# Early loads and Q projections in another order, copies of x also on ScalarE, and a new order table, in a cached attention kernel on one core

## The chip, the core and the metric

The kernel runs on one core of a Trainium2 chip. The core has TensorE (PE, matrix multiplications), VectorE (DVE), ScalarE (ACT), GpSimd (POOL) and SyncE (SP, which here issues all transfers). They run side by side and wait for each other on semaphores. TensorE writes into PSUM, which has eight banks; VectorE and ScalarE copy from there into SBUF. The metric is device time in microseconds (us) of one execution; lower is better. A profile is a recording of one execution.

## The reference: two attention blocks with a cache

Two independent problems, A and B, of the same shape, whose results are put side by side:

```python
q = (x @ wq).reshape(B, Sq, Hq, Dh).transpose(0, 2, 1, 3)
k = jnp.repeat(k_cache, rep, axis=1)          # rep = 2
v = jnp.repeat(v_cache, rep, axis=1)
scores = jnp.einsum("bhqd,bhkd->bhqk", q, k) * (Dh ** -0.5)
p = softmax(scores, axis=-1)
o = jnp.einsum("bhqk,bhkd->bhqd", p, v)
out = o.transpose(0, 2, 1, 3).reshape(B, Sq, Hq * Dh) @ wo
```

B = 16 batches, Sq = 80 new positions, D = 576, Hq = 32 query heads on Hkv = 16 key heads, Sk = 512 cached positions, Dh = 128. All inputs are bf16. K and V are 16 x 16 x 512 x 128 each, per problem.

## The kernel before

**Units.** The work is cut into 128 units, 64 for each problem. A unit is one batch and four key heads (eight query heads, so 640 query rows on 4 x 512 keys). Eight batches make a half. Eight units with the same key heads and the same half are an octet (`goct`); octets are walked in pairs, a unit of one and a unit of the other in turn.

**Steps of a unit.** K is loaded for two units at a time by a transposing transfer (L637, `ldk`), V for one unit (L641, `ldv`). Scores are five matmul groups: four of 128 query rows, one for each key head (L684, `qk`), and one that takes the 32 rows left over of each of the four heads at once, on four 32-column parts of the array (L671, `qkr`). Each group fills one PSUM bank. VectorE takes the negated maximum (L693, `max`), ScalarE the exponential with the row sum (L697, `exp`), VectorE the reciprocal (L703, `rcp`), GpSimd multiplies (L706, `nrm`). For two units together TensorE then transposes the probabilities in 64-row parts of the array (L741, `tr`); VectorE or ScalarE copies them out (L758, L759, L767, L768: `ptev`, `prev`); the product with V follows (L789, `pv`) and is copied out (L803, `oev`). The output projection with `wo` (L835, `op`) runs over 16 heads at a time; its first part goes to an accumulator (L847), the second is added (L864) and stored (L870).

**Q projection.** For each octet there are eight steps `m`: four batches and two query heads each (`m` 0 to 3 for the first four batches, 4 to 7 for the others). A head's projection is four matmuls over the first 512 rows of `wq` (L557, `qp`) and one 64-row matmul over the last 64 rows (L570, `qt`; two heads sit on the two 64-row parts). The result is scaled and copied out (L582 on ScalarE, L583 on VectorE: `qev`). `wq` of the first two octets is loaded in four pieces of 256 columns (L526, `ldwa`), the rest whole; the last 64 rows come by two loads more (L530, `ldwt`).

**x.** In problem A, x is loaded as rows in two parts for each half (L400, `ldx`: blocks of 128 rows, three and two), transposed by TensorE block by block (L421, `xtr`) and copied out by VectorE (L426, `xev`). GpSimd repeats its last 64 columns (L408, `xrp`); they are transposed (L439, `xt`) and copied (L443, `xe`). In problem B a transposing transfer does most of it, and only the last 64 columns are loaded as rows (`ldxs`), transposed (L476, `xtt`) and copied in three instructions (L481 to L483, `xte`).

**The order.** Every operation is added with a name, the resources that it reads and writes, and a stream. Within a stream, operations keep the order of their keys. The order across streams is the table `ORDER`: one letter for the next operation of a stream (streams sorted by name), an apostrophe ahead of it where an operation that may run on VectorE or ScalarE (`alt=EV`) takes ScalarE, and a digit for the PSUM bank where a bank is taken. Each engine executes its operations in the order of that table. Waits follow from the resources. A load (a name that begins with `ld`) also waits for the TensorE operation that stands last ahead of it in the table:

```python
            if op.eng == "pe":
                last_pe = op
            elif op.paced and last_pe is not None:
                deps[id(last_pe)] = last_pe
```

All loads and stores are issued by SyncE, one after another. There are six places for K and six for V (`NK`, `NV`), 16 for probabilities, two for `wq`.

In the table before, the transfers ahead of the first K are a piece of `wq`, the first part of x, a piece of `wq` of octet 1, two `ldwt`, a piece, an `ldwt`, the second part of x, an `ldwt`, and three pieces: twelve. The second K load stands behind two pieces and a part of x, the third behind the other part of x and two V loads. Ahead of the first score matmul, TensorE has five blocks of x, eight `qp` of octet 0 and four of octet 1.

Of the kernel before, what the change touches and what calls it, by code (L numbers as in the profile page):

```python
# [7 lines left out]
F32 = mybir.dt.float32  # L8
# [26 lines left out]
X2K = 6.0  # L35
# [5 lines left out]
EV = ("dve", "act")  # L41
# [10 lines left out]
W4 = 2  # L52
# [10 lines left out]
1f6f2id7pmqmpnd0d5emppBACme'B'Amf3g1f4f7d6k0d5pqCpmnmef3f2'A'Bd1k6f5MpCppMpmmmd4k0f6k7eMMCpvvvvwOwvOvvvg37m'A'  # L63
Bmqh5012qnz'yh6ial4f3k0f5'z'ynxLpCCMpc1cf6c2cc4l7cm'um't'tf3c2icd0f1f4pLpCuppmmmd7ef2f5d3m'BCAppvvvvwvvvwvd1me
g67A'Bmqh3420Fh1nzf5f4qCpypC'yf6'xFd1nd2emzpc3cf5c7c'Am't'umif0c1d4cf7d6CppwvvvvvvwmtCpBmef1ac3c'Av'Bmh5042vpu
mf7ph3g16'y'z'xmyqf5b0c4cf7f3nqpCzCpn'tmic1cd6ic4f2cc5bcpupmmm'r'uCtCvvvwvvwvvvf3f1ad4ef2d0f7pppApm'Bmd3imeh45
61amBAh2'z'y'xig70zf3qf5f1'yFf4aic6cpnmc2Fcc7ctCqpCpp'u'tic6cb2f7'unmmbf0f5d6f1mpCrppCpmd2mmeg47d3wvvvwvvvvvBq
Amd0eh6521Bn'Aih0qy'zf4xp'yn'zf3f5f6d0c2Cpcc1cm't'uc7cc4cf2f1mCptCpppm'umvvwvvvwvmb7f3d5f4bd6ppCrmmd2mvveeg13B
'A'ABqh0475h2ib6qyy'z'xnn'zg07CCqqnac1f2bf5f3cc4pnwvvvvmrppmcf7d6d0f5ef2mpCupm'AmpBCc4cf7c3cf6ad5vvwvm't'ud2vp
tpmeh4310mBACzh7'y'xf6f2f4'zf5c1cipCytppmc3c'umc7cc0cif6b1tCpp'ummmd2f3f0iiibaf6d4d5pCpprmmvvwvvvvvvwmd7eeh163  # L70
0'BABh2A'yg74xg15q'z'zn'yf3c6cb0c7cqqqCtpn'unnmc2cf4f6bc7cf1Ctppp'ummmf2f3b5pCrbf6f1d7d4mprppCmvvvvwvvwvvd2mmd
0eeh5631CA'B'Ah4Bz'yag72'xf5'z'yqpf0ic3cc1f6cf4n'tmc7qppCpmb3f5cf0bCuptpvwvwvnmmc2f1cd6f4d7mCprpvvvvvd5m'umd0m
eaeh4123ACz'B'B'A'yih7g06'y'zf5Jf4xqc1f2cf3Jc7cinb0qpupCppn'tmmmf6bc7iCpvvvmcf4f1d2c3cf5mptpCpd6d7mvvwvwvvmd4m
ureeh0531CBC'A'Baiih2'z'A'yf4b6f7ypxpm'zmf0f2bc4cf5c1cGpCppum'r'tmvvwvvc3cf0d4f6d7f1c2icpppCum'tmmd3mwvvvvd5ee
h2160A'A'B'zBh4yg37'xg12'z'yqqnc5cf0b6c4f3ca'tnpCCqpmnmc5cf7bf1f3c0cqpuptpC'rmmn'umd4b6f7d5f2f0id3bpppCmwvvvvw
vvvvmmrd7eaieh0612'B'BAACh4'z'yg35xqf7'y'zJGif6nc1f0cc2cf4qCtppc1n'umcc3icb2f7'umtppCpmmf3d5d6f0md1f4JbpCppmmv
vvvvvvwwrCmd3eeh2407'AvBByh6'A'z'y'zag35xqf1f2c6cc4f7cf0nqCtpppb3n'ummd4f5c6f1cc2ipptCpmmmmbf6f7id0cd5pCpmvwvv
vvvvwvrCumad1eeh2367A'A'BBh4'zf0'yif1f5'z'yf3xppc6cc7m'tmcCupc2cc0cf7f4b6f1pCpvwvvwv'tmm'ud5d3f2ibd0mpppCmmm'r
vvvvd7eeah6412A'B'Bh3Ay'zg70'xg65'zqc4cf1c2cnqqpCuqb7nn'ym'tnbc6f3cf2rpCpc0b4f1iacf7i'tmm'uf6f5d2d0f3Cppmvvvwv
vmppCmbd7mpCrmd6vwvveeh3145'Ah2CBBy'A'z'y'zg70xqqf1iif3nc2cf4c5f6cnpppm'umc7cb0f1ppttCmmbf5f3Fd4ac2f6mpd7cd1pC  # L80
pmmwvvvvvwvvvurmd5eeh6023A'B'ABCyh4'zg75'xvf0'z'yqf6f2c1cc4f3caiinppqCpup'tmnc7mcb1c0cf5f4mmtCppmvvbif7d3f2d5F
d6pCprummmd4vwvvwvveeh7102CCBy'A'Ah5f6'B'z'y'zb3f7xppmmc2f1cf0f5bf6d4Fc7ppppCtmmcd0vvvvvvwm'r'umf5c2cf1iec7cd6
# [12 lines left out]
cc6cf1b5mputCmd6f4f7bimmCpppsd2d3mvvvvvwvvwvmmd0eieh4751DA'A'BBh6'yg02x'zg34'z'yqc7cc5f6cn'tc1cf0b7qqptpCn'umm
nvwvf1f2d5c6cbaf0f3ipqCCpummf6b1spCppnmmbf4d7d3vwvvvvvmspmd1eeh0624CBh7'A'A'B'zyg35'xf1'zf0yqc7ncc6cf2Cptpp'uf
4f3c7mmpmqpCmnmb6DDbcf1Fc2f4cFd5f0ptpCpmvvvwvwvvvvd3sumiiad1md7eeh2046'BCCBz'A'Ah3'yg17'xf0'z'yqpf5nmc4cc6f2f3
cppqpub1mmnf0pmbif2d5c6f7DcmpCsCpvvvvwvwvvvmc3cf1d0d2tpum'tmd7eeh4163CAA'Bh5a'y'y'xf2f0Bzppmmb7if4f6c1cbf5CpzC
psp'tmmc3f2cc1cid0f6Cpp'umm'tc3Dcf7d5d2pvwvwvvvvvvd1'ummeeh7436'B'A'Bh5i'zg01Ayg27z'y'xqaf6f4pnqmpnmf5b3c0bf6c
f1qsCpppCqCvwvwvvvn'tmmc4cb2c0cbf3f6utCppnmc5d0f7iid1d4cpuvvv'rmmmd2eeh5736B'A'Bh1'z'yg02CAxqf4f7ac5'y'zncFf1c  # L100
6cf3qpup'tc0b5cDf6mnmpCpmmf4bd7c2iiaf3if1tpCpmd0cd6mCppmmwvvvvvvvwvd4Crueeh3152B'A'zAh0yxg76'z'y'Bf3f1qqpnc5cf
2f0c4cb7Cpppnmmm'umbc3f6Ctrpcf1d5f4f2c7d0mpmcd6pCpmutmid1vvvwwvvvvvaeeh2743'BAACBh0F'zf5'yf1f7'z'yf6xpCpmc4cc2
cc0cf3d5ia'umtppCptmmc4b1f2cf0f6d7ppCp'umvwvvwvvvvvmbd4immrd3eeh1260A'B'ABh5zg47zqqg32'y'x'yf1f6c0cb5bn'tnpqpC
qric7cnmmc3f0cf5c1f4ppCp't'umf6cd7f3nmmpCupCvvvvvwvvwvmb0f2d1d5Diabpmm'rd6eeh0432i'BABACzh1v'y'x'z'yg76ib0f2qq
pnnmc3f1cc7f5cptCpc6f4cf2bf3im'umptpCmf1d7mppmmf4c6cd5d2pCCrumd3evvvwvvwvveh1604G'ABBzAh5'yg73a'xf1qCqf6c0'z'y
cc2f4cc5n'tnpuppf7f0iJcf2b3mmptpCpmmvwvvvvwvf1bf6d5d4c7cmmppCum'rmvvd0d2Jaeeh3761A'A'Biiih5'zBCyf4'xf0f3'z'ypp
# [185 lines left out]
def bass_concat_heads__gqa_block_cached__gqa_block_cached__near_ridge_kernel(  # L292
# [27 lines left out]
    with ExitStack() as es:  # L320
# [32 lines left out]
        def R(res, ver):  # L353
            return (res, ver)
# [594 lines left out]
```

## Time and profile before

| what | value |
|---|---|
| median of 3 runs | 718.41 us (718.02 to 719.71) |
| the profiled execution, its own time | 720.19 us |
| its span, first to last instruction | 718.3 us |
| TensorE matmuls busy | 704.7 us (98%) |
| ScalarE busy | 647.4 us (90%) |
| VectorE busy | 617.8 us (86%) |
| GpSimd busy | 431.9 us (60%) |
| read from HBM, written | 87.65 MB, 2.95 MB |

The span leaves out 1.9 us of the execution's own time. Busy time of TensorE is counted to modelled ends of matmuls, and neighbouring ones overlap. Rows of the timeline have the start and length in us, the engine, the line, the operation, what is written and read, how many instructions were merged, and in brackets the idle time ahead with what ended it. Rows of the table of stretches have the stretch, its length, then busy time and number of instructions of PE, PEld (weight loads), DVE, ACT and POOL, the granted TensorE clock, the busy share of the transfer engines and GB/s.

### The profile page before, as it was taken

Reading aid. Unit: us, or ns where it says so; the run is one execution under the profiler, and the core shown is the slowest. Engines: PE = TensorE matmul, PEld = TensorE weight load, DVE = VectorE, ACT = ScalarE, POOL = GpSimd, SP = SyncE. Lnnn points to the kernel's source line nnn. Section 1 sums busy time; section 2 is a strip of 40 time slices with the busy share of each in tenths; the row PEclk is TensorE's granted clock in tenths of the full one; section 3 lists DMA queues with packets and bytes.
Section 4 is the critical chain, followed back from the end, with each engine's and each line's share of the span. In section 5 each row is a group of like instructions: output and inputs, shape, how many; then the busy total and the mean of one; then the engine's idle time right before and its main releaser. Section 6 shows DMA issues by size and latency. Waiting matters only on the chain.

```text
span 718.3 us, 26080 instructions
## 1 busy us (share of the span) xinstructions
PE 704.7 (98%) x10820; PEld 511.7 (71%) x10820; DVE 617.8 (86%) x1345; ACT 647.4 (90%) x1766; POOL 431.9 (60%) x650
## 2 busy tenths in 40 slices
PE   7899999999999999999999999999999999999998
PEld 4566677777776777767677777777777777777777
DVE  2899898989798888888988899898888998899894
ACT  2999989999999899989999998999999999999893
POOL 0467657656566575565755576565755655566573
DMA  9999996999998989999989889999978999799871
GB/s 224 238 276 241 261 263 141 216 252 242 249 255 230 238 205 250 217 269 248 214 201 222 214 188 255 243 251 246 262 150 204 239 240 243 183 231 207 184 206 51
DMA packets 374165, 160.70 MB, mean 224 GB/s; under 512 B 278560, under 2 KB 370976, under 8 KB 374048
## 3 DMA queue, kind: packets, MB, share of 16 engines
q1 hardware_dynamic: 374048, 159.05, 95.1%
q8 instruction: 85, 1.39, 0.8%
q14 instruction: 32, 0.26, 0.1%
HBM read 87.65 MB, written 2.95 MB: 126 GB/s over the span
## 4 chain that ended last, share of the span: by engine, by line
PE 89%; DMA 7%; DVE 1%; SPq 1%; issue 1%; ACT 0%; POOL 0%
PE ps L835 21%; PE ps L789 18%; PE ps L557 18%; PE ps L684 15%; PE ps L741 10%; PE ps L671 4%; PE ps L570 3%; DMA kT<-in_A_k_cache_dram 3%; DMA kT<-in_B_k_cache_dram 2%; DVE negmax L693 1%; DMA xst<-in_B_x_dram 1%; DMA acc<-in_A_x_dram 1%; DMA wq_sb<-in_A_wq_dram 1%; DMA out_dram<-osb 1%; ACT p_sb L697 0%
## 5 line engine op out<-in xcount | busy, mean ns | idle before, releaser
L706 POOL TENSOR_SCALAR p_sb<-p_sb,rinv 128x512 bf16<-128x512 bf16 x640 | 430.1, 692 | 266.3 <-DVE rinv L703 265.8
L697 ACT ACTIVATE p_sb<-ps,negmax 128x512 bf16<-128x512 f32 x640 | 438.0, 711 | 20.1 <-DVE negmax L693 17.8
L693 DVE TENSOR_REDUCE negmax<-ps 128x1 f32<-128x512 f32 x640 | 411.1, 678 | 21.8 <-PE ps L684 14.0
L789 PE MATMUL ps<-pT,v_sb 128*128 128x160 bf16 x2048 | 182.1, 233 | 1.0 <-issue 1.0
L789 PEld LDWEIGHTS ps<-pT,v_sb 128*128 128x128 bf16 x2048 | 152.8, 98 | 37.9 <-DVE pT L768 4.9
L835 PE MATMUL ps<-wo_sb,oT 128*128 128x288 bf16 x1280 | 179.8, 286 | 0.0
L684 PE MATMUL ps<-kT,qT 128*128 128x512 bf16 x512 | 167.5, 380 | 2.4 <-DMA kT<-in_A_k_cache_dram 1.0
L557 PE MATMUL ps<-xT,wq_sb 128*128 128x320 bf16 x1024 | 165.4, 299 | 2.8 <-issue 1.3
L835 PEld LDWEIGHTS ps<-wo_sb,oT 128*128 128x128 bf16 x1280 | 123.2, 98 | 40.8 <-ACT pT L758 0.6
L697 ACT ACTIVATION_READ_ACCUMULATOR p_sb<-ps,negmax 128x1 f32 x640 | 145.3, 227 | 0.0
L557 PEld LDWEIGHTS ps<-xT,wq_sb 128*128 128x128 bf16 x1024 | 97.9, 98 | 46.8 <-issue 2.5
L758 ACT COPY pT<-ps 128x512 f32<-128x512 f32 x190 | 103.4, 603 | 7.1 <-PE ps L741 5.2
L741 PEld LDWEIGHTS ps<-ident,p_sb 64*128 64x128 bf16 x5120 | 82.4, 95 | 9.8 <-POOL p_sb L706 1.6
L583 DVE TENSOR_SCALAR qT<-ps 128x320 bf16<-128x320 f32 x124 | 56.5, 484 | 37.5 <-PE ps L570 37.4
L741 PE MATMUL ps<-ident,p_sb 64*128 64x64 bf16 x5120 | 86.3, 190 | 0.5 <-ACT p_sb L697 0.3
L582 ACT ACTIVATE qT<-ps 128x320 bf16<-128x320 f32 x132 | 51.5, 437 | 29.0 <-PE ps L570 28.7
L803 DVE CAST oT<-ps 128x320 bf16<-128x320 f32 x140 | 66.2, 477 | 3.4 <-PE ps L789 2.7
L684 PEld LDWEIGHTS ps<-kT,qT 128*128 128x128 bf16 x512 | 45.1, 97 | 31.8 <-ACT pT L758 8.3
L803 ACT CAST oT<-ps 128x320 bf16<-128x320 f32 x116 | 50.0, 442 | 5.0 <-PE ps L789 4.6
L759 DVE COPY pT<-ps 128x1024 bf16<-128x1024 bf16 x66 | 44.4, 683 | 4.7 <-PE ps L741 4.6
L703 DVE RECIPROCAL rinv<-rowsum 128x3 f32<-128x3 f32 (+1 forms) x256 | 39.6, 159 | 3.9 <-ACT p_sb L697 3.7
L671 PE MATMUL ps<-kT,qT 128*32 128x512 bf16 x512 | 37.6, 383 | 1.5 <-DVE rinv L703 0.6
(31 smaller groups left out, 149.2 us busy)
## 6 DMA issues: line engine op xcount, KB each, us to landing
v_sb<-in_A_v_cache_dram SPq DMA_DIRECT2D x64, 512.0 KB, 5.4
v_sb<-in_B_v_cache_dram SPq DMA_DIRECT2D x64, 512.0 KB, 5.1
wo_sb<-in_A_wo_dram SPq DMA_DIRECT2D x8, 576.0 KB, 5.4
wo_sb<-in_B_wo_dram SPq DMA_DIRECT2D x8, 576.0 KB, 5.3
wq_sb<-in_B_wq_dram SPq DMA_DIRECT2D x4, 1024.0 KB, 7.4
out_dram<-osb SPq DMA_DIRECT2D x40, 72.0 KB, 4.2
wq_sb<-in_A_wq_dram SPq DMA_DIRECT2D x8, 256.0 KB, 4.0
wq_sb<-in_A_wq_dram SPq DMA_DIRECT2D x2, 1024.0 KB, 8.2
```

The lines of the kernel that those rows point to most:

```text
L557: last = e.matmul(ps[:, vbq[h].phys, QO:QO + 320], lhsT=wq_sb[:, wsl, ck, hi * 128:(hi + 1) * 128], rhs=xT[:, half, ck, n0:n0 + 320], star ...
L583: return e.tensor_scalar(dst, src, SCALE, None, op0=AluOpType.mult)
L671: last = e.matmul(ps[32 * g4:32 * g4 + 32, vb_.phys, :], lhsT=qT[:, qsl_, bl_, g4 * 160 + 128:g4 * 160 + 160], rhs=k_of(U_, g4), start=Tru ...
L684: return e.matmul(ps[:, vb.phys, :], lhsT=qT[:, qsl, bl, gl * 160:gl * 160 + 128], rhs=k_of(U, gl), start=True, stop=True)
L693: return e.tensor_reduce(negmax[:, si:si + 1], ps[:, vb.phys, :], axis=AX.X, op=AluOpType.max, negate=True)
L697: return e.activation(p_sb[:, psl, :], ps[:, vb.phys, :], AF.Exp, bias=negmax[:, si:si + 1], scale=1.0, accum_out=rowsum[:, ss, k:k + 1])
L706: return e.tensor_scalar(p_sb[:, psl, :], p_sb[:, psl, :], rinv[:, ss, k:k + 1], 1.0, op0=AluOpType.mult, op1=AluOpType.mult)
L741: last = e.matmul(dst, lhsT=p_sb[64 * h:64 * h + 64, psl2[i_][k_], j * 128:(j + 1) * 128], rhs=ident[64 * h:64 * h + 64, 64 * h:64 * h + 6 ...
L758: return e.copy(dst.bitcast(F32), ps[:, vb.phys, :].rearrange("p (j n) -> p j n", j=4))
L789: last = e.matmul(ps[:, vo.phys, off:off + 160], lhsT=v_sb[:, vs, gl, j * 128:(j + 1) * 128], rhs=pT[:, pts, j, :, 32 * gl:32 * gl + 32], ...
L803: return (e.copy if en == "act" else e.tensor_copy)(dst, src)
L835: last = e.matmul(ps[:, vb.phys, 0:DC], lhsT=oT[:, sp_ * (HH // 2) + i, rb * 128:(rb + 1) * 128], rhs=wo_sb[:, 2 * c3 + sp_, i, :], start= ...
```

## The change

- The two first octets get streams of their own for `qp`, `qt`, `qev` and `ldwt` (`Q0`, `Q1` and so on), so that the table can put octet 0 and octet 1 in any order against each other. The transposes of x get a stream for each half.
- Copies of x out of PSUM (`xev`, `xe`, and for problem B `xte`) may run on ScalarE, which copies pairs of bf16 as 32-bit words. `xte` becomes two operations, 0 for the upper 64 partitions and 1 for the lower.
- The table is another one throughout, and more letters are known.

By the new table, SyncE begins with both parts of x, two pieces of `wq`, two `ldwt`, a piece of octet 1, two pieces; then the first K (tenth). Behind it stand a piece, two `ldwt`, two pieces, the second K, then a V load, a part of x, the third K, the other part of x, two V loads, the fourth K. TensorE has five blocks of x, twelve `qp` of octet 0 and two of octet 1 ahead of the first score. One copy of a block of x, one `xe` and both first `xte` stand on ScalarE.

```diff
-LETTERS = "abcdefghijklmnopqrstuvwxyzABCDEFGHIJKLMNOPQ"
+LETTERS = "abcdefghijklmnopqrstuvwxyzABCDEFGHIJKLMNOPQRSTUVWXYZ!#$%&(),-."
 ORDER = """
-HKIHHHIKIoEj2oNNHHIk6ak4k0l5EMLMMd1d0d2el7d3Iek4d6I'Bd5ALBMed4Kd0aKied3'A'B'B'Ad7k2d1ed5eMBA'A'A'Bf0pg3iaf5f4d
...
-                      stream="xrp%d" % half)
+                      stream="xrp")
...
-                    def em_xev(e, half=half, blk=blk, vb=vb):
-                        return e.tensor_copy(xT[:, half, 0:4, blk * 128:(blk + 1) * 128],
-                                             psb[:, vb.phys, 0:512].rearrange("p (c n) -> p c n", c=4))
+                    def em_xev(e, en, half=half, blk=blk, vb=vb):
+                        dst = xT[:, half, 0:4, blk * 128:(blk + 1) * 128]
+                        if en == "act":
+                            return e.copy(dst.bitcast(F32), ps[:, vb.phys, 0:256].rearrange("p (c n) -> p c n", c=4))
+                        return e.tensor_copy(dst, psb[:, vb.phys, 0:512].rearrange("p (c n) -> p c n", c=4))
...
-                          name="xtr%d" % rb, stream="X", alloc=[vb])
+                          name="xtr%d" % rb, stream="X%d" % half, alloc=[vb])
...
-                          name="xev%d" % rb, stream="xev")
+                          name="xev%d" % rb, stream="xev", alt=EV)
...
+                    dst = xT[:, half, 4, k0 * 128:k1 * 128]
+                    if en == "act":
+                        return e.copy(dst.bitcast(F32), ps[:, vb.phys, 0:64 * (k1 - k0)])
+                    return e.tensor_copy(dst, psb[:, vb.phys, 0:128 * (k1 - k0)])
...
-                      name="xt%d.%d" % (half, part), stream="X2", alloc=[vb])
+                      name="xt%d.%d" % (half, part), stream="Y%d" % half, alloc=[vb])
...
-            def em_xev2(e, half=half, vb=vb):
-                e.tensor_copy(xT[0:64, half, 4, :], psb[0:64, vb.phys, 0:NROW])
-                e.tensor_copy(xT[64:128, half, 4, 128:NROW], psb[64:128, vb.phys, 0:NROW - 128])
-                return e.tensor_copy(xT[64:128, half, 4, 0:128], psb[64:128, vb.phys, NROW - 128:NROW])
+            def em_xev2(e, en, r, half=half, vb=vb):
+                copy = e.copy if en == "act" else e.tensor_copy
+                if r == 0:
+                    return copy(xT[0:64, half, 4, :], psb[0:64, vb.phys, 0:NROW])
+                copy(xT[64:128, half, 4, 128:NROW], psb[64:128, vb.phys, 0:NROW - 128])
+                return copy(xT[64:128, half, 4, 0:128], psb[64:128, vb.phys, NROW - 128:NROW])
...
+            for r in range(2):
+                S.add("dve", k_ + X2K + 0.5 + 0.1 * r, lambda e, en, r=r, f=em_xev2: f(e, en, r), reads=[R(vb, 0)],
+                      writes=[R(("xt", half, b_, r), 1) for b_ in range(NRT)], name="xte%d.%d" % (half, r), stream="xte%d" % r, alt=EV)
...
-                              dsem="d_wt%d" % wsl, name="ldwt%d.%d" % (goct, r), stream=strm if goct < W4 else "wt")
+                              dsem="d_wt%d" % wsl, name="ldwt%d.%d" % (goct, r), stream="wt%d" % goct if goct < 2 else "wt")
...
-                          name="qp%d.%d.%d" % (goct, m, h), stream="Q", alloc=[vbq[h]])
+                          name="qp%d.%d.%d" % (goct, m, h), stream="Q" if goct > 1 else "Q%d" % goct, alloc=[vbq[h]])
...
-                      writes=[R(v_, 0) for v_ in vbq], name="qt%d.%d" % (goct, m), stream="QT")
+                      writes=[R(v_, 0) for v_ in vbq], name="qt%d.%d" % (goct, m), stream="QT" if goct > 1 else "QT%d" % goct)
...
-                          name="qev%d.%d.%d" % (goct, m, h), stream="qev%d" % h, alt=EV)
+                          name="qev%d.%d.%d" % (goct, m, h), stream="qev%d" % h if goct > 1 else "qev%d%d" % (goct, h), alt=EV)
```

(The lines of the two tables themselves are left out.)

More of the change, by code (lines that the diff above doesn't have):

```diff
@@ L66 @@
[L66 to L70, printed above, removed]
@@ L546, in bass_concat_heads__gqa_block_cached__gqa_block_cached__near_ridge_kernel @@
                 xr = [R(("xT", half, b_), prob) for b_ in blks]
-                xtr = [R(("xt", half, b_), prob) for b_ in blks]
+                xtr = [R(("xt", half, b_, r_), prob) for b_ in blks for r_ in range(2)]
                 us = sess[goct, m]
```

135 lines of the change are left out of this document (69 added, 66 removed).

## The prediction

> **What bounds the kernel now.** I read the page's busy line first, then a table of stretches, then TensorE's own timeline with the reasons of its idle time, then SyncE's.
>
> ```profile
> PE 704.7 (98%) x10820; PEld 511.7 (71%) x10820; DVE 617.8 (86%) x1345; ACT 647.4 (90%) x1766; POOL 431.9 (60%) x650
> ```
>
> TensorE is the bound, with ScalarE not far behind. Only time in which TensorE stands, or changes of its own work, can be won. The table of stretches (busy us per engine) says where it stands:
>
> ```profile
> 0.00:4.90 4.90, 3.21 (x8) 1.04 (x8) 0.33 (x2) 1.28 (x1) 0.73 (x7) 1.00 0.61 187
> 4.90:17.00 12.10, 10.34 (x86) 6.25 (x86) 4.30 (x11) 2.51 (x6) 0.59 (x2) 1.00 1.05 235
> 17.00:26.50 9.50, 7.27 (x53) 3.54 (x52) 7.71 (x17) 8.75 (x25) 3.50 (x6) 1.00 1.16 210
> 26.50:37.00 10.50, 9.67 (x164) 6.67 (x165) 9.94 (x23) 9.51 (x27) 6.38 (x11) 1.00 1.05 274
> 37.00:66.20 29.20, 29.03 (x465) 19.86 (x466) 27.35 (x59) 28.71 (x82) 19.58 (x31) 1.00 1.09 256
> 66.20:345.00 278.80, 276.09 (x4241) 200.55 (x4240) 243.33 (x528) 260.14 (x710) 172.88 (x258) 1.00 1.02 235
> 345.00:356.00 11.00, 10.23 (x194) 6.75 (x192) 10.26 (x23) 9.99 (x29) 6.49 (x10) 1.00 1.16 241
> 356.00:715.70 359.70, 358.81 (x5632) 266.99 (x5624) 314.12 (x685) 326.48 (x891) 221.76 (x331) 1.00 0.90 212
> ```
>
> Idle are 1.69, 1.76, 2.23, 0.83 and 0.17 us up to 66.2, so 6.7 of the whole 13.6. Of these 1.24 lie before the first matmul; 5.4 are left. A wait costs somewhat more than the idle time shown, because neighbouring matmuls overlap: a score matmul is 0.38 long but two of them are 0.59, so the second starts 0.21 after the first and 0.17 is hidden. With eleven waits that is some 1.9 more: the first 66 us lose about 7.3 us. The clock column is 1.00 in every stretch.
>
> What TensorE waits for there, from its timeline:
>
> ```profile
> 1.24 3.21 PE L373 MATMUL ps<-wo_sb 128*128 128x512 bf16 x8 [1.24 <-DVE wo_sb L366]
> 4.94 0.83 PE L421 MATMUL ps<-ident,acc 128*128 128x128 bf16 x12 [0.49 <-DMA acc<-in_A_x_dram]
> 7.05 1.80 PE L557 MATMUL ps<-xT,wq_sb 128*128 128x320 bf16 x12 [1.11 <-DVE xT L426]
> 9.71 0.28 PE L439 MATMUL ps<-ident,acc 128*128 128x128 bf16 x2 [0.61 <-POOL acc L408]
> 16.98 0.38 PE L684 MATMUL ps<-kT,qT 128*128 128x512 bf16 x1
> ...
> 26.49 0.59 PE L684 MATMUL ps<-kT,qT 128*128 128x512 bf16 x2 [1.04 <-DMA kT<-in_A_k_cache_dram]
> 36.99 0.59 PE L684 MATMUL ps<-kT,qT 128*128 128x512 bf16 x2
> 45.70 0.38 PE L684 MATMUL ps<-kT,qT 128*128 128x512 bf16 x1
> ```
>
> The rows at 16.98, 26.49, 36.99 and 45.70 are the first scores from the first, second, third and fourth load of K (two units each). SyncE's rows for the same loads:
>
> ```profile
> 8.11 6.71 SPq L637 DMA_TRANSPOSE kT<-in_A_k_cache_dram  x1
> ...
> 16.59 7.77 SPq L637 DMA_TRANSPOSE kT<-in_A_k_cache_dram  x1
> ...
> 26.09 7.04 SPq L637 DMA_TRANSPOSE kT<-in_A_k_cache_dram  x1
> ...
> 34.35 6.91 SPq L637 DMA_TRANSPOSE kT<-in_A_k_cache_dram  x1
> ```
> ```profile
> 26.09 10.77 DMA kT<-in_A_k_cache_dram
> ```
>
> The chain of waits runs through the third of them: 10.77 us from issue, landed at 36.86, used at 36.99. So K, behind all else in one queue, paces the first 46 us, and TensorE fills in with Q projections.
>
> **The change, part by part.** The two order tables can be read letter by letter (streams sorted by name), which gives each engine's sequence; counts below are from them.
>
> *Start.* x of half 0 goes to the head of the queue (issue 0.79 instead of 1.30; it landed 3.6 after issue, at 4.9, so now by 4.4). The warm-up, not x, then ends last: eight matmuls from 1.24, the next start at about 4.65. Three transposed blocks follow 0.22 apart.
>
> ```profile
> 5.36 0.42 DVE L426 COPY xT<-ps 128x512 bf16<-128x512 bf16 x1 [0.78 <-PE ps L421]
> 5.97 0.36 DVE L443 COPY xT<-ps 128x384 bf16<-128x384 bf16 x1 [0.19 <-PE ps L439]
> 6.25 0.74 DVE L426 COPY xT<-ps 128x512 bf16<-128x512 bf16 x2
> ```
> ```profile
> wq_sb<-in_A_wq_dram SPq DMA_DIRECT2D x8, 256.0 KB, 4.0
> L582 ACT ACTIVATE qT<-ps 128x320 bf16<-128x320 f32 x132 | 51.5, 437 | 29.0 <-PE ps L570 28.7
> L758 ACT COPY pT<-ps 128x512 f32<-128x512 f32 x190 | 103.4, 603 | 7.1 <-PE ps L741 5.2
> ```
>
> The copies of the three blocks now go VectorE, ScalarE, VectorE, with the tail copy (0.36) behind them. A ScalarE copy of 128x256 words isn't in the trace: the rows above bound it, at most 0.60 and hardly under half of that; I take 0.40. VectorE's two end at 4.65+0.42+0.74 = 5.85 and set the end either way, so the bounds come to nothing. The first piece of wq, third in the queue as another piece was before (issue 1.84 + 4.0), is there at 5.85 to 6.2. First Q projection at about 6.0 instead of 7.05: 1.05 won. The wait of 0.61 for GpSimd (x's tail) goes too, as that transpose now stands behind ten other projections.
>
> *To the first K.* Ahead of its first load there are now nine loads, not twelve (a wq piece and two tail weights less, about 0.6 of SyncE each): issue near 6.3.
>
> ```profile
> DMA to landing us min/median/max: 6.1/8.7/12.7
> ```
>
> With the median it lands at 15.0. TensorE has 14 projections (four matmuls each, 0.54) ahead of the first score instead of 12. From the first projection it took 9.93 before; less 0.7 for the wait that is gone, plus 1.1 for two projections, plus 0.2 for a transpose moved behind, less 0.4 because tail projections now stand in pairs, makes 10.1. Pieces three and four of wq are needed at 9.95 and 11.2, and 1.9 MB at the 235 GB/s of that stretch come in at about 10.4: 0.2 to 0.8 of waiting, I take 0.5. First score at 16.6 (before 16.98) with K there.
>
> *To the second K.* Five small loads (0.56 each) after the first K, issue near 15.8, against 16.59. The bytes between the two loads are nearly the same (1920 against 1968 KB), and that took 9.5 us from use to use: landing 24.5, by issue time 25.6. TensorE has 1.54 us more work there (two projections and two tails more, a transpose less), and its waits of before (1.04 and smaller ones, 2.65 of the 9.51) leave 6.87 + 1.54 = 8.4: it arrives at 25.0. Use at 25.3, 1.2 earlier, with 2.24 us more work done by then: 3.4 won.
>
> *Third and fourth K.* One part of x and one V load are moved behind the third K, in all 1968 KB after the second instead of 2336, so 10.5 us shrink to 8.9 by bytes: landing 33.9, or 35.4 if it takes 10.77 from issue. TensorE arrives at about 33.5 (7.4 of work, up to 1.0 for GpSimd's normalising). Use at 34.5, 0.79 more work done: 3.3 won, 2.4 to 3.9 by the bounds. The fourth comes out at 43.9 with 1.64 more done, 3.4. The fifth and sixth K now stand ahead of the first two wo loads, so what little is lost on them today goes. **First term: −3.6 us (−2.0 to −4.8).**
>
> *Changes of tile shape.* The 64-row matmuls (L570, L741) and the column-tiled ones (L671) stand between full ones. The tables have 221 such changes before and 229 after.
>
> ```profile
> 12.44 1.25 PE L557 MATMUL ps<-xT,wq_sb 128*128 128x320 bf16 x8
> 13.62 0.31 PE L570 MATMUL ps<-xT,wt 64*128 64x320 bf16 x2
> 13.86 0.58 PE L557 MATMUL ps<-xT,wq_sb 128*128 128x320 bf16 x3
> ```
>
> Eight matmuls of 0.136 are 1.09 and the next starts after 1.18: 0.1 for the change. It is paid on TensorE with nothing to hide it. **Second term: +0.8 us.** [...]
>
> *x of problem B.* Its tail is copied in two streams on either engine, and the transpose stands about 13 us of TensorE work behind its load instead of 4.5.
>
> ```profile
> 350.26 0.44 PE L476 MATMUL ps<-ident,xst 128*128 128x128 bf16 x5 [0.33 <-DMA xst<-in_B_x_dram]
> 351.86 0.39 PE L684 MATMUL ps<-kT,qT 128*128 128x512 bf16 x1 [0.39 <-DVE xT L483]
> ```
>
> The first waits for the load, the second for the three copies (one bank). With the hidden 0.17 of each they cost 1.1 to 1.2. **Third term: −1.0 us** (0 to −1.2).
>
> *The rest.* The table is new throughout, but total work is the same, copies are shared out almost as before (ScalarE 8 instructions more in 1125), and of the 4.4 idle us outside the start, 2.3 are three pauses in which nothing shown is waited for. I take 0, from −1.5 to +2.
>
> Sum: −3.6 + 0.8 − 1.0 = −3.8. The profiled span 718.3 becomes 714.5, its own time 720.19 becomes 716.4. That run stood 1.8 above the median shown, 718.41; taken off the median: **714.6 us**.
>
> **Rivals.** *ScalarE takes the pace* (0.20). For it:
>
> ```profile
> 30.00:66.00 36.00, 35.45 (x601) 24.57 (x601) 34.09 (x76) 35.46 (x101) 23.38 (x35) 1.00 1.09 256
> ```
> ```profile
> 18.12 0.69 ACT L697 ACTIVATE p_sb<-ps,negmax 128x512 bf16<-128x512 f32 x1 [0.29 <-DVE negmax L693]
> ...
> 30.81 0.69 ACT L697 ACTIVATE p_sb<-ps,negmax 128x512 bf16<-128x512 f32 x1
> ```
>
> From 30 to 66 it stands for 0.5 us of 36. Between the rows at 18.12 and 30.81 lie 14 exponentials, of which it idles some 1.9. It can only come earlier by a sooner first exponential (about 0.4) and less of those 1.9, and six more Q copies stand ahead of the 64th exponential (six times 0.44, about 3 us with what goes along, given back by the 79th). If half of the 1.9 stays, the first term is −1.3 and the time is 718.41 − 1.5 = 716.9. Against it: with the second K 1.2 us sooner the idle time ahead of the 11th exponential should go.
>
> *Loads released too near their use* (0.10), the one that ends slower. Every load waits for the matmul group ahead of it in the table. Added up with the start-to-start times of TensorE's rows (0.54 for four projection matmuls, 0.21 for a score and so on), the new table leaves 6.6 us of work between release and use of unit 6's V (before 9.1), 5.7 for unit 66's V (before over 12), 7.0 for the wq of octet 13 (before 10.7).
>
> ```profile
> DMA to landing us min/median/max: 3.7/5.2/10.7
> ```
> ```profile
> DMA to landing us min/median/max: 2.8/5.4/8.8
> ```
>
> The first is V's in problem A and B together, the second wq's. At the medians all are in time; it decides from landings over those figures. At the worst they cost (10.7 − 6.6) + (10.7 − 5.7) + (8.8 − 7.0) = 10.9; at two thirds of that 7.3, and 718.41 − 3.8 + 7.3 = 721.9.
>
> **Chances.** My forecast 0.70. A measurement of this kernel tells 0.3%, 2.2 us, from no change: faster is under 716.25, slower over 720.6. The forecast case ends in a small part within it (first term at −2), so faster 0.66, same 0.25, slower 0.09. Its own range by the bounds is 711.3 to 717.5; to hold eight in ten with the ScalarE case in it I take 711.3 to 718.8.
>
> **What would show it.** Right: first L557 matmul near 6.0; second K used near 25.3 and third near 34.5, at more projections done; idle of TensorE up to 66 us down from 6.7 to 3 or 4; no wait at the xst transpose. ScalarE's case: its 14th exponential still near 30.8. The slow case: weight loads of L789 or L557 waiting for DMA. Wrong altogether: new waits of several us after 66 us, since nothing above prices them.

## The result, and the profile after

| | before | after |
|---|---|---|
| median, same chip | 719.18 us (716.25 to 723.97) | 715.51 us (713.86 to 717.11) |
| ratio of the times, 95% interval | 1 | 0.9943 (0.9919 to 0.9966) |
| the profiled execution, its own time | 720.19 us | 715.38 us |
| its span | 718.3 us | 712.3 us |

The forecast was 714.6 us, so a fall of 3.8 us; the medians fell by 3.7. On a second chip (below) the same kernel stood at 0.997 (0.995 to 0.999), 2.1 us. So by the medians the change makes the kernel faster by 2 to 4 us, and the forecast lies at the upper end of that.

The busy line of the page after, then the table of stretches (same columns and borders as before):

```profile
PE 703.7 (99%) x10820; PEld 511.9 (72%) x10820; DVE 614.7 (86%) x1337; ACT 647.0 (91%) x1774; POOL 432.6 (61%) x650
```
```profile
0.00:4.90 4.90, 3.66 (x11) 1.41 (x12) 0.27 (x1) 1.28 (x1) 1.02 (x7) 1.00 0.59 177
4.90:17.00 12.10, 11.46 (x99) 7.02 (x96) 3.55 (x10) 3.59 (x10) 0.29 (x1) 1.00 1.05 230
17.00:26.50 9.50, 9.48 (x65) 4.57 (x64) 9.22 (x20) 8.90 (x27) 4.11 (x7) 1.00 1.13 227
26.50:37.00 10.50, 9.84 (x152) 6.13 (x153) 10.50 (x25) 10.50 (x30) 8.31 (x13) 1.00 1.14 285
37.00:66.20 29.20, 29.20 (x489) 20.40 (x487) 28.58 (x62) 29.01 (x85) 19.96 (x32) 1.00 1.15 251
...
345.00:356.00 11.00, 11.00 (x173) 8.02 (x171) 10.27 (x24) 10.82 (x31) 7.59 (x12) 1.00 1.21 222
```

TensorE's idle time up to 66.2 us is 1.24, 0.64, 0.02, 0.66 and 0, together 2.6 us where it was 6.7, and the stretch at 345 us has none where it had 0.77. Its timeline at the first Q projections, at the first scores from the first four K loads, and at the transpose of x in problem B:

```profile
4.63 1.01 PE L421 MATMUL ps<-ident,acc 128*128 128x128 bf16 x12
6.16 0.72 PE L565 MATMUL ps<-xT,wq_sb 128*128 128x320 bf16 x4 [0.52 <-DVE xT L429]
...
16.44 0.59 PE L692 MATMUL ps<-kT,qT 128*128 128x512 bf16 x2
...
24.90 0.61 PE L692 MATMUL ps<-kT,qT 128*128 128x512 bf16 x2
...
33.64 0.38 PE L692 MATMUL ps<-kT,qT 128*128 128x512 bf16 x1
...
42.96 0.38 PE L692 MATMUL ps<-kT,qT 128*128 128x512 bf16 x1
...
353.81 0.44 PE L481 MATMUL ps<-ident,xst 128*128 128x128 bf16 x5
```

And SyncE's rows of those four K loads, issued at 6.04, 16.68, 23.67 and 31.68 instead of 8.11, 16.59, 26.09 and 34.35:

```profile
6.04 6.42 SPq L645 DMA_TRANSPOSE kT<-in_A_k_cache_dram  x1
16.68 5.76 SPq L645 DMA_TRANSPOSE kT<-in_A_k_cache_dram  x1
23.67 6.28 SPq L645 DMA_TRANSPOSE kT<-in_A_k_cache_dram  x1
31.68 7.59 SPq L645 DMA_TRANSPOSE kT<-in_A_k_cache_dram  x1
```

**How the 6.0 us of span split up.** In what follows *lost time* is TensorE's time less the sum of its own steps, where a step is the start-to-start time of neighbouring matmuls in rows without a wait (0.136 us for a projection, 0.216 for a score, 0.069 for a product with V, 0.123 for an output matmul, 0.096 more for a change of tile shape). The steps sum to 696.8 us before and 697.6 after, so the work grew by 0.8. Lost are 17.4 us before and 10.7 after, in one recording of each:

| stretch | lost before | lost after | difference |
|---|---|---|---|
| up to 80 us | 7.56 | 3.0 | −4.6 |
| 100 to 120 us | 0.1 | 1.7 | +1.6 |
| 300 to 330 us | 2.05 | 0.42 | −1.6 |
| 340 to 360 us | 1.69 | 0.27 | −1.4 |
| 400 to 420 us | 0.1 | 1.18 | +1.1 |
| all else | 5.9 | 4.1 | −1.8 |

The two rows with a plus are in the main new waits for a K load, which take back part of the gain:

```profile
102.98 0.61 PE L692 MATMUL ps<-kT,qT 128*128 128x512 bf16 x2 [0.78 <-DMA kT<-in_A_k_cache_dram]
...
417.03 0.71 PE L679 MATMUL ps<-kT,qT 128*32 128x512 bf16 x8 [0.98 <-DMA kT<-in_B_k_cache_dram]
```

### The profile page after: what moved, and what is told of

It is laid out like the page before. It is cut to its first block, busy times and chain, and to the rows that moved or that the text cites. A ratio compares the mean times of both kernels' runs of the same rounds, so it can differ in the third digit from the quotient of the medians.

```text
span 712.3 us, 26078 instructions
## 1 busy us (share of the span) xinstructions
PE 703.7 (99%) x10820; PEld 511.9 (72%) x10820; DVE 614.7 (86%) x1337; ACT 647.0 (91%) x1774; POOL 432.6 (61%) x650
## 3 DMA queue, kind: packets, MB, share of 16 engines
q8 instruction: 85, 1.39, 0.8%
HBM read 87.65 MB, written 2.95 MB: 127 GB/s over the span
## 4 chain that ended last, share of the span: by engine, by line
PE 92%; ACT 5%; DMA 2%; DVE 1%; issue 0%
PE ps L843 21%; PE ps L797 19%; PE ps L565 18%; PE ps L692 15%; PE ps L749 10%; PE ps L679 4%; ACT p_sb L705 4%; PE ps L578 3%; DMA kT<-in_B_k_cache_dram 2%; ACT pT L766 1%; ACT qT L590 1%; PE ps L373 1%; PE ps L421 0%; ACT pT L775 0%; ACT oT L811 0%
## 5 line engine op out<-in xcount | busy, mean ns | idle before, releaser
L797 PE MATMUL ps<-pT,v_sb 128*128 128x160 bf16 x2048 | 184.7, 233 | 0.5 <-issue 0.4
L797 PEld LDWEIGHTS ps<-pT,v_sb 128*128 128x128 bf16 x2048 | 154.4, 98 | 39.1 <-ACT pT L775 2.9
L565 PE MATMUL ps<-xT,wq_sb 128*128 128x320 bf16 x1024 | 167.5, 299 | 0.7 <-DVE xT L429 0.5
L705 ACT ACTIVATION_READ_ACCUMULATOR p_sb<-ps,negmax 128x1 f32 x640 | 150.5, 235 | 0.0
L766 ACT COPY pT<-ps 128x512 f32<-128x512 f32 x182 | 99.6, 602 | 6.3 <-PE ps L749 4.4
L811 DVE CAST oT<-ps 128x320 bf16<-128x320 f32 x135 | 64.3, 481 | 9.0 <-PE ps L797 8.8
L811 ACT CAST oT<-ps 128x320 bf16<-128x320 f32 x121 | 53.3, 453 | 1.9 <-PE ps L797 1.7
L767 DVE COPY pT<-ps 128x1024 bf16<-128x1024 bf16 x74 | 49.3, 685 | 4.8 <-PE ps L749 4.3
```

The source lines that it names most:

```text
L565: last = e.matmul(ps[:, vbq[h].phys, QO:QO + 320], lhsT=wq_sb[:, wsl, ck, hi * 128:(hi + 1) * 128], rhs=xT[:, half, ck, n0:n0 + 320], star ...
L705: return e.activation(p_sb[:, psl, :], ps[:, vb.phys, :], AF.Exp, bias=negmax[:, si:si + 1], scale=1.0, accum_out=rowsum[:, ss, k:k + 1])
L766: return e.copy(dst.bitcast(F32), ps[:, vb.phys, :].rearrange("p (j n) -> p j n", j=4))
L797: last = e.matmul(ps[:, vo.phys, off:off + 160], lhsT=v_sb[:, vs, gl, j * 128:(j + 1) * 128], rhs=pT[:, pts, j, :, 32 * gl:32 * gl + 32], ...
L811: return (e.copy if en == "act" else e.tensor_copy)(dst, src)
```

## Experiments

Each ratio is to the kernel before, timed on the same chip. The letters behind a load's name are octet and piece (or part), as in the code: `ldwa0.2` is the third piece of `wq` of octet 0.

### Which part of the start makes the gain: order of loads or order of projections

The two tables differ in the first 21 loads and in TensorE's order between them. Either was put in without the other. The first kernel is the changed one with the loads of before:

```diff
 first 21 loads
-x0.0 x0.1 wa0.0 wa0.1 wt0.0 wt0.1 wa1.0 wa0.2 wa0.3 K0 wa1.1 wt1.0 wt1.1 wa1.2 wa1.3 K2 v0 x1.0 K4 x1.1 v1
+wa0.0 x0.0 wa1.0 wt0.0 wt0.1 wa0.1 wt1.0 x0.1 wt1.1 wa0.2 wa0.3 wa1.1 K0 wa1.2 wa1.3 x1.0 K2 x1.1 v0 v1 K4
```

> The changed kernel, with its first 21 loads (to the third K and the V of unit 1) put back into the order of the kernel before, at the same places of the table; everything else as changed. Queue theory (the place of K in SyncE's queue is what the start won): K lands as before, near 16.9, 26.4 and 36.9 us, while TensorE has 15.3, 23.7 and 31.1 us of its own work ahead of these; so it has lost about 5.8 us at the third K where the changed kernel has lost 2.5. Time: the changed kernel's plus 3.3, ratio to the kernel before about 0.999. Projection theory (the order and number of Q projections ahead of K won it, the loads follow anyway): no slower than the changed kernel, ratio about 0.994.

Measured: 1.0063 (1.0039 to 1.0087), worse than either theory. The projections that were moved ahead need the second part of x, which now comes late, and the clock falls to 0.50 during the wait. Then the loads are held up in turn, because each waits for the TensorE operation ahead of it in the table: SyncE stands 6.6 us at a piece of `wq`, and the first K is issued at 14.12, where the kernel before had it at 8.11. A row of TensorE's timeline in this kernel, and its table of stretches, in which the column behind the five engines is the granted clock:

```profile
9.12 0.61 PE L421 MATMUL ps<-ident,acc 128*128 128x128 bf16 x4 [1.90 <-DMA acc<-in_A_x_dram]
```
```profile
4.90:8.00 3.10, 1.55 (x16) 0.99 (x16) 0.85 (x2) 0.37 (x1) 0.34 (x1) 0.99 1.08 264
8.00:11.00 3.00, 1.88 (x12) 1.42 (x13) 0.42 (x1) 0.00 (x0) 0.29 (x1) 0.50 0.70 197
11.00:14.00 3.00, 3.00 (x18) 1.53 (x15) 0.69 (x2) 0.00 (x0) 0.00 (x0) 0.50 0.01 2
14.00:16.00 2.00, 2.00 (x15) 1.18 (x12) 0.89 (x2) 0.77 (x2) 0.00 (x0) 0.80 0.47 131
```

The first score comes at 22.58 instead of 16.44. The second kernel is the reverse, the table of before with the loads of after:

> The kernel before, with its first 21 loads in the order of the changed one, and nothing else of the table changed. Queue theory: the third and fourth K land near 33.5 and 43 us as in the changed kernel, TensorE has 30.3 and 38.7 us of work ahead of them, so it loses about 4.2 us by the fourth K instead of 7.0: 2.8 faster than before, ratio about 0.996. Projection theory: TensorE runs dry sooner and gains nothing, ratio 1.000.

Measured: 1.0087 (1.0053 to 1.012). TensorE's order of before needs the first part of x of half 1 before the second K is used, and that part now stands behind it. From TensorE's timeline in this kernel:

```profile
28.65 0.61 PE L421 MATMUL ps<-ident,acc 128*128 128x128 bf16 x4 [3.46 <-DMA acc<-in_A_x_dram]
```

The clock is at 0.50 from 27.70 to 37.94 in this recording. Both theories fall as they were put. The order of loads and the order of projections are worth nothing alone; each makes the other wait.

### The place of the K loads alone

The changed kernel, with only the three K loads pushed back to their place of before. x and wq come in time:

```diff
-x0.0 x0.1 wa0.0 wa0.1 wt0.0 wt0.1 wa1.0 wa0.2 wa0.3 K0 wa1.1 wt1.0 wt1.1 wa1.2 wa1.3 K2 v0 x1.0 K4 x1.1 v1
+x0.0 x0.1 wa0.0 wa0.1 wt0.0 wt0.1 wa1.0 wa0.2 wa0.3 wa1.1 wt1.0 wt1.1 K0 wa1.2 wa1.3 x1.0 K2 x1.1 v0 v1 K4
```

> The changed kernel with only the three K loads of the start put back in SyncE's queue to where they stood before (behind the seven weight pieces that stand ahead of them in the order of before); the loads of x and the order of TensorE stay those of the changed kernel. Queue theory: the first K load lands near 16.9, the second near 26.4, the third near 36.9 us instead of 12.5, 22.4 and 30.0, so the third K is waited for at 33.6 us, 3.3 us lost over the changed kernel (up to 6 if a pause lets the granted clock fall), ratio to before about 0.999. Rival (the projections ahead make the whole gain and K is not what is late): no more than 0.5 us lost, ratio 0.994 to 0.995.

Measured: 1.0012 (0.9991 to 1.0033), where the changed kernel itself stood at 0.997 (0.995 to 0.999) on that chip, 3.2 us less by the medians. The loss comes at the first K and not at the third. From TensorE's timeline in this kernel:

```profile
18.51 0.60 PE L692 MATMUL ps<-kT,qT 128*128 128x512 bf16 x2 [1.71 <-DMA kT<-in_A_k_cache_dram]
```

TensorE lost 1.88 us there. Not only the place in the queue made this K late: at the two `ldwt` ahead of it SyncE stood 3.3 us for TensorE, by the rule of the table, so it was issued at 10.27 and landed at 18.46, later than in the kernel before (8.11 and 16.85). All behind it moved by about as much, and the third K, used at 35.60, landed just in time, at 35.47. (The landings that the expectation gives for the changed kernel, 12.5 and 22.4, are the ends of SyncE's rows; the first two K loads land there at 14.48 and 24.60.) The seventh K's first score comes at 75.2 us, where the changed kernel has it at 73.2 to 73.4. So a later K costs, with the projections in their new order, and the rival falls; but the size is 1.8 to 2.0 us and not 3.3, and what the place in the queue costs without SyncE's waits is not shown. The rest of the difference lies past 200 us.

### The start alone, and the rest alone

> The first 805 operations of the changed table (to about 112 us), then the rest in the order of the kernel before, with PSUM banks given anew where needed. If the gain is made in the start: all of it but the wait at the x of problem B, so some 4 us faster than before (ratio 0.993 to 0.995), and that wait (about 1.2 us near 345) is back. If the rest of the table makes it: ratio 0.998 to 1.000. Changes of tile shape are 220 here against 229, worth 0.9 us by the row of the profile.

The first 805 operations (up to about 112 us) of the table after, then the order of before. Measured: 0.9993 (0.9966 to 1.0019). That is what was expected if the rest of the table makes the gain. By the recording the start kept its gain all the same (2.6 us lost up to 80 us), but this execution lost 2.9 us at 100 to 125 us, 1.4 of them waiting for K, the waits at x of problem B were back (1.5 us), and one pause with no reason shown was followed by half the clock. TensorE's timeline and the table of stretches of this kernel:

```profile
191.85 0.45 PE L797 MATMUL ps<-pT,v_sb 128*128 128x160 bf16 x4 [2.60 <-issue]
```
```profile
189.00:192.00 3.00, 0.40 (x7) 0.20 (x4) 1.37 (x3) 2.61 (x8) 0.00 (x0) 1.00 1.30 158
192.00:194.00 2.00, 2.00 (x15) 1.61 (x14) 0.95 (x3) 0.52 (x1) 0.38 (x1) 0.55 1.27 290
194.00:196.00 2.00, 2.00 (x12) 1.34 (x10) 0.91 (x2) 1.35 (x5) 0.98 (x2) 0.60 0.29 65
```

The reverse, the first 805 operations of before and then the order of after:

> The order of the kernel before up to about 112 us (its first 805 operations), and from there the order of the changed kernel. Theory that the start makes most of the gain: the 4.7 us lost up to 66 us are back, the wait of 1.2 us for x of problem B at 350 us stays away, so ratio to before about 0.997 to 1.000. Rival (the rest of the new order makes the gain): ratio 0.994 or lower.

Measured: 1.0033 (1.0008 to 1.0058), slower than either expectation. The start's loss is back (6.7 us up to 80 us, before 7.6, after 3.0), x of problem B costs nothing (the stretch from 345 to 356 us is busy throughout), and pauses with no reason shown at 218 and 317 us cost 2.25 and 1.62 us. This kernel differs from the changed one in the start alone, and on the same chip it takes 721.45 us against 716.07: 5.4 us, of which the recordings put 3.7 in the first 80 us. So the start makes the gain, and no gain of the rest is seen beyond x of problem B. The sizes do not add up, though: by the times of the two halves nothing should have been won, and that the start alone shortens the kernel before is seen in lost time only. What varies between these kernels are the pauses and the waits for K.

### What a change of tile shape costs

Each `qt` of the octets from 2 on right behind its own `qp`, instead of two `qt` together: 335 changes of shape instead of 229, the same matmuls.

> The changed kernel, with the 64-row tail projection of every step of the octets from 2 on put right behind its own two projections, so that they no longer stand in pairs or next to the transposes: 335 changes of tile shape instead of 229. At 0.096 us a change, read from starts of matmuls, it is 10.2 us slower than the changed kernel, ratio to the kernel before about 1.008. [...] If the change of shape hides behind the weight load, 0: ratio 0.994.

Measured: 1.0107 (1.0074 to 1.014). Against the changed kernel's 0.9943 and 0.997 that is 9.8 to 11.8 us for 106 changes, 0.09 to 0.11 us each. (Its profile also has 3.4 us of waiting for a K load of problem B, and a granted clock of 0.72 from 368 to 374 us, so this is rather too much than too little.) The 0.1 us of the row holds.

### Two K loads sooner

The K loads that are waited for at 103 and 417 us, put ahead of one V load and of three (the text on record counts two and one):

```diff
-qk72 ... v14 K18 v15 ...  v71 v72 v73 v74 K76
+qk72 K18 ... v14 v15 ...  v71 K76 v72 v73 v74
```

> The changed kernel with two K loads put ahead in SyncE's queue: the one that is waited for at 103 us ahead of two V loads, the one that is waited for at 417 us ahead of one V load. Theory that the pacing of the loads (not bandwidth) makes these waits: 0.95 and 1.05 us go, the span falls by 1.5 to 2 us against the changed kernel, ratio to before about 0.992. Rival (the transfers are limited by the queue as a whole, so that the V loads become late in turn, or the time is given back to other waits): the same time as the changed kernel, 0.994.

Measured: 0.9998 (0.9973 to 1.0024), against 0.997 (0.995 to 0.999) for the changed kernel, so no gain, and rather a loss. Both waits for K are gone, and the rival came true at the first of them: the V load that it was put ahead of, issued at 97.6 instead of 90.7, is then late in K's stead. From TensorE's timeline in this kernel:

```profile
102.06 0.44 PE L797 MATMUL ps<-pT,v_sb 128*128 128x160 bf16 x4 [1.55 <-DMA v_sb<-in_A_v_cache_dram]
...
419.73 0.61 PE L679 MATMUL ps<-kT,qT 128*32 128x512 bf16 x7
420.85 0.39 PE L679 MATMUL ps<-kT,qT 128*32 128x512 bf16 x1 [0.50 <-issue]
```

At 417 us the K load landed at 414.3 and the wait went, and a pause with no reason shown followed within the same group.

### The changed kernel again

> The changed kernel as it is, timed beside the three others on the same chip. All theories: ratio to the kernel before about 0.994, span 712 to 713, lost time of TensorE (its span less the sum of its instructions' own steps) about 10.7 us, with 0.95 us lost at 103 us and 1.05 us at 417 us, both waiting for a K load.

Measured: 0.997 (0.995 to 0.999), 716.07 us. Its profile lost 11.2 us. The wait for K at 103 us is there again (0.75 us lost); at 417 us K landed at 417.42 and TensorE idled only 0.16, where the recording above has 0.98. It lost 1.1, 0.85 and 1.33 us at 215, 248 and 314 us, where the recording above lost 1.03, 0.17 and 0.35. The kernel is the same, the places are the same, and the lengths differ.

### Pauses that follow the instruction stream

The places of the pauses showed a pattern. Counted through all matmuls of the kernel before, those that come behind its three pauses with no reason shown have the numbers 1099, 3115 and 4627: 16 times 126 and 12 times 126 apart. The page counts, in its list of transfer queues,

```profile
q8 instruction: 85, 1.39, 0.8%
```

85 packets and 1.39 MB, 16.4 KB to a packet. TensorE has 10,820 matmuls and as many weight loads, 21,640 instructions; if the queue is TensorE's alone, 85 packets make 255 instructions to a packet, some 127 matmuls. The page does not say whose queue it is; that the pauses are multiples of 126 apart speaks for TensorE's. The trace has a start for each of these packets, and each of the three pauses ends 2.5 to 2.6 us after one. In the other kernels, too, pauses lie at numbers that leave 91 to 95 over 126. So do waits that the profile gives to ScalarE: at 215 us in the changed kernel the wait of 1.03 us ends 2.5 us after a packet, at a number that leaves 94.

Test: move the stream, and leave the order of the work as it is. The 8 warm-up matmuls of 512 columns became 32 of 128, in the same time:

```diff
-NWARM = 8
+WARM = ((32, 0),)
...
-            for _ in range(NWARM):
-                last = e.matmul(ps[:, vw.phys, :], lhsT=ones, rhs=warm, start=True, stop=True)
+            for n_, w_ in WARM:
+                for _ in range(n_):
+                    last = e.matmul(ps[:, vw.phys, 0:w_ * 256], lhsT=ones, rhs=warm[:, 0:w_, :], start=True, stop=True) if w_ else \
+                        e.matmul(ps[:, vw.phys, 0:128], lhsT=ones, rhs=warm[:, 0, 0:128], start=True, stop=True)
```

> The changed kernel with the 8 warm-up matmuls of 512 columns replaced by 32 of 128 columns (the same columns in all): every later matmul of TensorE stands 24 places further on in its instruction stream, and nothing else is changed. Code theory: the pauses of TensorE past 66 us follow its instruction stream. 10,820 matmuls and as many weight loads make 21,640 instructions, and the profile counts 85 packets of 16 KB on the instruction queue, so 126 to 128 matmuls to a packet; in the runs so far the pauses lie at matmuls whose number leaves 91 to 95 over 126, and end 2.3 to 2.8 us after a packet. They then lie again at such numbers, 24 matmuls earlier in the order of the work than before: none at the matmuls that paused in the changed kernel at 215, 248, 313 us (they now leave about 118 over). Rival (the order itself makes these waits: ScalarE and VectorE are late there, as the rows of the wait at 215 us say): the pauses stay at the same matmuls of the work, 0.9 to 1.1 us at 215 us. The time by the first may fall or rise by 2 us (other places, not fewer), by the second it is that of the changed kernel, 0.994 to 0.997.

Measured: 0.9965 (0.9942 to 0.9987), 714.84 us. The matmuls that paused at 215, 248 and 313 us run without a gap. From TensorE's timeline in this kernel, the rows around the first of them, and the row of the new pause spoken of below:

```profile
214.65 0.71 PE L567 MATMUL ps<-xT,wq_sb 128*128 128x320 bf16 x4
215.19 0.81 PE L694 MATMUL ps<-kT,qT 128*128 128x512 bf16 x3
215.84 0.41 PE L845 MATMUL ps<-wo_sb,oT 128*128 128x288 bf16 x2
...
537.58 0.31 PE L799 MATMUL ps<-pT,v_sb 128*128 128x160 bf16 x2 [1.14 <-issue]
```

and the largest pause is now at 537 us, 2.4 us after a packet, at a number that leaves 95. A second pause of 1.04 us, at 274 us, ends 2.7 us after a packet at a number that leaves 100, outside the 91 to 95 expected. The code theory holds for the three pauses that went, and that ScalarE and VectorE were late at these places falls. Two more waits of 1.11 and 0.89 us (80 and 113 us) are at other numbers; by their rows the first is for VectorE and the second for a V load.

The same with 12 warm-up matmuls of 256 columns and 8 of 128:

> The same with 12 warm-up matmuls of 256 columns and 8 of 128, 20 in all: every later matmul 12 places further on. Code theory: pauses at numbers that leave 91 to 95 over 126, thus 12 matmuls earlier in the order of the work than in the changed kernel; the matmuls that paused there now leave 104 to 107 over and run without a pause. Rival: the pauses stay at the same matmuls of the work. Time within 2 us of the changed kernel by the first, the same by the second.

Measured: 0.992 (0.9892 to 0.9948), 712.31 us (711.09 to 713.25), the fastest here, though the interval of its ratio overlaps that of the changed kernel on the first chip. The profile lost 8.7 us; of the waits of half a microsecond and more past 66 us two are left, 0.99 and 0.74 us, both at numbers that leave 93 and both 2.5 us after a packet. The waits for K at 103 and 417 us are missing as well, 2.0 us against the first recording of the changed kernel, so the pauses are not the whole of what this kernel won. The first wait left stands in this kernel's timeline as a wait for ScalarE:

```profile
115.36 0.39 PE L694 MATMUL ps<-kT,qT 128*128 128x512 bf16 x1 [0.83 <-ACT oT L813]
```

The kernel before with the same warm-up:

> The kernel before with the warm-up of 12 matmuls of 256 and 8 of 128 columns, so that its later matmuls too stand 12 places further on in TensorE's instruction stream. Tells whether the 0.992 that this shift gave the changed kernel is the shift's alone. Code theory: the pauses of the kernel before at 88, 218 and 318 us (matmuls that leave 91 over 126; 0.68, 1.14 and 0.93 us lost) are gone and others come at numbers that leave 91 to 95; the start loses its 6.7 us up to 66 us as before; ratio to the kernel before between 0.997 and 1.003, so that against the changed kernel with the same shift it stays 4 to 6 us behind. Rival (the shift helps any order by some 4 us): ratio 0.994 or lower.

Measured: 1.0021 (1.0001 to 1.004). Its three pauses are gone and one of 1.05 us came at 151 us, at a number that leaves 91, 2.7 us after a packet. The start lost 6.7 us up to 80 us (7.6 without the shift), and x of problem B cost more (2.9 us at 340 to 360 us). So the shift does not help any order, and with it the change is worth about 1% (0.992 against 1.0021, on two chips).

### The copies of x on ScalarE

> The changed kernel with the two copies of x out of PSUM that went to ScalarE back on VectorE, order unchanged: tells what that part of the change is worth. Theory that it shortens the way to the first Q projection: that projection about 0.3 us later (6.5 instead of 6.16 us) and the span 0.3 us longer, ratio 0.995 to 0.998. Rival (the copies are hidden behind the wq piece, or an engine of its own saves nothing): the first Q projection unchanged at 6.2 to 6.6 us.

Measured: 0.9964 (0.994 to 0.9988), the first Q projection at 6.22 us; in recordings with the copies on ScalarE it comes at 6.10 to 6.63, and once at 7.42, where a piece of wq was late. No difference can be told: the rival holds, this part of the change is worth at most a few tenths.

## Why the prediction was right, and where its terms were off

**Start, −3.6 us (−2.0 to −4.8) forecast, −4.6 measured (−4.4 with the second recording of the changed kernel).** The mechanism holds: with K back in its old place 1.8 to 2.0 us more are lost, with the old start 3.7 more. Its steps, forecast and measured:

| step | forecast | measured |
|---|---|---|
| first Q projection | 6.0 | 6.16 |
| first K issued, first score | 6.3, 16.6 | 6.04, 16.44 |
| second K issued, used | 15.8, 25.3 | 16.68, 24.90 |
| third K used | 34.5 | 33.64 |
| fourth K used | 43.9 | 42.96 |
| copy of a block of x on ScalarE | 0.40 | 0.37 |

Two terms were mis-sized. For wq's pieces three and four 0.5 us of waiting was put in, and 0.29 came. For the stretch to the third K "up to 1.0 for GpSimd's normalising" was kept; lost time between the uses at 24.90 and 33.64 is 1.3, with a wait of 0.61 for a copy of Q as its largest part, and the landing, put at 33.9 to 35.4, was not waited for. The copies' sum in the prediction is 5.81 and not 5.85, which changes nothing. It did not ask what the loads or the projections are worth alone: each alone costs 4 to 6 us.

**Changes of tile shape, +0.8 forecast.** By the steps the work grew by 0.8, and 106 more changes cost 0.09 to 0.11 us each. Right.

**x of problem B, −1.0 forecast (0 to −1.2).** The transpose at 353.81 has no wait and the stretch lost 1.4 us less. With the rest of the old order the waits are back, with the rest of the new one they are gone. Right, a little small.

**The rest, 0 forecast (−1.5 to +2).** It came out at −0.8 in the recording: the sum of two new waits for K (+2.0), fewer pauses, and small waits that went. This is where the prediction had no mechanism. Of 4.4 us it said that 2.3 were "three pauses in which nothing shown is waited for" and took them as given. The matmuls behind all three have numbers that leave 91 over 126, and with 12 matmuls more ahead of them the pauses were gone from these places; the new table has other work at such numbers. Together with the larger gain at the start and at x of problem B that makes a span that fell by 6.0 where 3.8 was forecast. The medians show 3.7 of it: the execution's own time fell by 4.8 only, since 3.1 us of it lie outside the span where 1.9 did, and the profile of before stood 1.0 us above its median. So the mechanism of the start, of the shapes and of x was right, but that the number agrees to 0.1 us is luck: on the second chip it is 2.1. The stated range is not what the terms give, either: their ends add up to 711.7 and 719.2, where the prediction has 711.3 to 717.5 by the bounds.

**The rivals.** ScalarE does not take the pace: its 14th exponential, in ScalarE's timeline after the change, starts at 28.64, not near 30.8.

```profile
28.64 0.76 ACT L705 ACTIVATE p_sb<-ps,negmax 128x512 bf16<-128x512 f32 x1
```

Loads too near their use: of the weight loads it named, a single one, of a projection, waits 0.3 us for a transfer in the changed kernel. But K, which the prediction had not looked at past 46 us, is 0.8 to 1.0 us late twice.

## What to carry to other kernels

Loads and the work that they feed are one order: move a load ahead only together with the work that can use it, and check what now stands behind it (here either alone came out at 1.0063 and 1.0087). Two K loads put ahead of V loads won nothing here (0.9998 against 0.997): a wait of 0.78 us for K became one of 1.55 us for V. Where a long, straight-line kernel shows pauses of about a microsecond that nothing explains, number the engine's instructions and look whether the pauses are a fixed count apart (here multiples of 126 matmuls). Here 12 or 24 matmuls more at the start moved them: with 12 the changed kernel came out faster (0.992), and the kernel before did not (1.0021), so comparisons of two orders carry that as noise.

## What the hardware showed that was not expected

- **Many pauses end 2.2 to 2.95 us after a packet of the instruction queue.** Of nearly 60 waits of half a microsecond or more past 66 us, in all recordings of this study, 35 do, at matmul numbers that leave 88 to 100 over 126, which is one number in ten. They make some 38 of some 60 us. Many recordings share an order, so places count several times; the test is that the pauses at 215, 248 and 313 us left their places when 24 matmuls more stood ahead of them. What makes such a pause is not shown, nor why the kernel before has three of them at 85 packets; that the profile names ScalarE (0.87 us idle at 215 us) or nothing as the reason does not tell them from other waits.
- **Some waits came with half the clock, and the length of the wait does not tell which.** After the wait of 2.60 us that ended at 191.85 the granted clock was 0.50 from 192.18 to 195.60. With the loads of before it fell to 0.50 at 7.96, within a wait of 1.90 us; projection matmuls that start 136 ns apart at full clock started 267 ns apart there. A pause of 2.09 us that ended at 218.97, in the kernel with the start of before and the rest of after, left it at 1.00:

```profile
218.97 0.57 PE L565 MATMUL ps<-xT,wq_sb 128*128 128x320 bf16 x3 [2.09 <-issue]
```

The half clock lasted 3.41 us in the first case, 6.83 with the loads of before (from 7.96) and 10.24 with the loads of after (from 27.70, within a wait of 3.46 us), each close to a multiple of the first. The table of stretches has one row ahead of the fall at 7.96, two for the start of after (ahead of the fall and behind it), and two for the start of before (with the pause of 2.09 us and behind it):

```profile
4.55:7.96 3.41, 1.75 (x17) 0.99 (x16) 0.91 (x3) 0.37 (x1) 0.34 (x1) 1.00 1.08 272
...
188.77:192.18 3.41, 0.81 (x13) 0.59 (x10) 1.60 (x3) 2.84 (x8) 0.00 (x0) 1.00 1.28 179
192.18:195.60 3.42, 3.42 (x20) 2.44 (x18) 1.86 (x4) 1.75 (x5) 1.36 (x2) 0.50 0.85 193
...
216.00:219.00 3.00, 0.91 (x9) 0.58 (x7) 1.66 (x4) 2.56 (x8) 0.00 (x0) 1.00 1.01 154
219.00:221.00 2.00, 2.00 (x15) 1.33 (x14) 1.21 (x3) 0.48 (x1) 0.34 (x1) 1.00 1.12 338
```

Nor do TensorE's busy times in these stretches tell it: 1.75 and 0.81 of 3.41 us stood ahead of falls, and with 0.91 of 3.00 us the clock stayed at 1.00. What decides is not shown. Where the clock fell, the wait cost more than its length: 2.60 us at 191.85 cost some 4.5 by lost time.
